# Linear attention into a two-of-four expert attention layer on one Trainium2 core: three batches in flight instead of two, with TensorE's instructions in program order

## The chip, the core and the metric

The kernel runs on one core of one Trainium2 chip. The metric is the device time of one execution in microseconds, less is better. The core has a matrix engine (TensorE: PE for matmuls and transposes, PEld for its weight loads), VectorE (DVE), ScalarE (ACT), GpSimd (POOL) and SyncE (SP), which here issues all the DMAs. [...] 

## The reference

Eight batches of 576 tokens. The first half is linear attention with 8 heads of 64, normalised per token and head; the second half is a mixture of four causal attention experts, of which each token uses the two with the largest logits.

```python
# q, k, v: (8, 8, 576, 64)
kv  = einsum('bhsd,bhse->bhde', k, v)
out = einsum('bhsd,bhde->bhse', q, kv)
x   = out / sqrt(mean(out*out, -1) + 1e-6) * g_norm      # -> (8, 576, 512)
logits = x @ w_gate                                      # 4 experts, the best 2 are kept
w = softmax over the two kept logits
for e in range(4):
    q, k, v = x @ wq[e], x @ wk[e], x @ wv[e]            # 512 -> 64
    a = causal_softmax(q @ k.T / 8)
    y += w[e] * (a @ v @ wo[e])                          # 0 where e was not kept
```

## The kernel before

The work goes batch by batch. The 576 tokens make five blocks, four of 128 and one of 64. Two Python generators emit a batch's instructions, and each `yield` is a place where the other generator may be advanced.

`stage1(b)` is the linear attention. `kv_pair` makes k^T v (`p_kv`, L179), `kv_copy` takes it from PSUM to SBUF (`kvx` on DVE, L187; `kv` on ACT, L188). `q_block` transposes q (`p_q`, L200, copied by DVE to `qT`, L205). The gate weights are folded into the same product (`p_kt`, `kvT`, `p_kg`). Then, block by block, `p_out` (L243) is q times kv; DVE copies it to `o_sb` (L250), ACT squares it (`sq`, L254), and DVE sums the squares per head (`ms`, L260). When all five blocks are done, DVE computes the reciprocal square root for all tokens at once, by a bit shift and four Newton steps of three small instructions each (L271 to L281). DVE forms the logits (`gl`, `lg`), and POOL multiplies the rows by the factor, one instruction per block (`x_tok`, L296). TensorE transposes each `x_tok` block (`p_x`, L307), and ACT copies it to `xT` (L312).

`stage2(b)` is the experts. It works out the gates on DVE (L322 to L341, with one ACT exponential), then `p_v` (L347, copied by DVE to `vext`), and for two pairs of experts the projections (`p_proj`, L365, cast by ACT to `qTp` and `kT`), the scores (`p_sc`, L393), their exponential on ACT (`PT`, L403), the causal mask on POOL (L408), the product with v (`p_O`, L445), the scaling by gate over row sum on DVE (`inv` and `osc`, L460 to L465), and the transposes of that (`p_OT`, L477, copied by ACT to `OT`). `final(b)` multiplies by wo (`p_y`, L501), ACT copies (`y`, L506) and SP stores (L507).

The matmul results share two sets of PSUM buffers: `big`, three of two banks (`p_out`, `p_proj`, `p_sc`, `p_O`), and `small`, two of one bank (`p_kv`, `p_q`, `p_kt`, `p_kg`, `p_x`, `p_v`, `p_OT`, `p_y`).

`weave` runs `stage2(b)` as the main stream and slips in `stage1(b + 1)` in proportion to costs that the generators yield. The part of `stage1` up to `p_out` is spread over 72% of `stage2`; the part from the normalisation on is held back to its last 8%. `final(b)` is emitted inside `stage2(b + 1)`. What the Python code emits is not yet the order of the engines: the framework's scheduler then orders each engine's instructions by readiness and priority. In the queues it makes, the normalisation of batch b + 1 and its `p_x` transposes stand between the last `p_O` of batch b and the first full `p_v` of batch b + 1.

The q, k and v tiles have two buffers; `load_qkv(b + 2)` is emitted at the start of round b. `kvx`, `lg8`, `ms` and `vext` also alternate between two copies; `o_sb` has one.

Of the kernel before, what the change touches and what calls it, by code (L numbers as in the profile page):

```python
# [10 lines left out]
FP32R = mybir.dt.float32r  # L11
BF16 = mybir.dt.bfloat16
# [6 lines left out]
def kernel(  # L19
# [13 lines left out]
    nc = tc.nc  # L33
    P = nc.NUM_PARTITIONS
    B, H, S, Dh = q.shape
    D = H * Dh
    E, _, Hd = moe_wq.shape
    assert (P, H, S, Dh, E, Hd) == (128, 8, 576, 64, 4, 64)
    NCH = D // P
# [25 lines left out]
    def small(shape, name, dtype=FP32):  # L65
        return ps1.tile(shape, dtype, tag="small", name=name)
# [121 lines left out]
            nc.scalar.copy(kv2[pp, :, hh * Dh : (hh + 1) * Dh], p_kv[pp, :, :])  # L188


    def stage1(b, res):
        qb, kb, vb = loads[b]
        qT = s1.tile([P, NCH, S], FP32, tag="qT", name="qT", bufs=1)
        kvb, kv2 = kvx[b % 2], kv2s[b % 2]
# [39 lines left out]
            q_block(i)  # L234
            yield 0.5

        xT = s1.tile([P, NCH, S], FP32R, tag="xT", name="xT")
        lg8, ms = lg8s[b % 2], mss[b % 2]

        for i, (t0, nt) in enumerate(blocks):  # L240
# [33 lines left out]
            out=y[:].bitcast(I32), in0=half[:], scalar1=-1.0, scalar2=float(0x5F3759DF),  # L274
            op0=AluOpType.mult, op1=AluOpType.add,
        )
        for it in range(4):
            u, w, y2 = tiny("u"), tiny("w"), tiny("y")
            nc.vector.scalar_tensor_tensor(out=u[:], in0=y[:], scalar=0.5, in1=y[:], op0=AluOpType.mult, op1=AluOpType.mult)
            nc.vector.tensor_tensor(out=w[:], in0=u[:], in1=m, op=AluOpType.mult)  # L280
            nc.vector.scalar_tensor_tensor(out=y2[:], in0=w[:], scalar=1.5, in1=y[:], op0=AluOpType.subtract, op1=AluOpType.mult)  # L281
            y = y2
        gl = blk.tile([P, NB * H, E], FP32, tag="gl", name="gl")
        nc.vector.tensor_tensor(
# [9 lines left out]
        for i, (t0, nt) in enumerate(blocks):  # L294
# [5 lines left out]
                op=AluOpType.mult,  # L300
            )
            xts.append(xt)
        yield 0.0
        for i, (t0, nt) in enumerate(blocks):
            p_x = small([P, NCH, P], "p_x")
            for c in range(NCH):
# [7 lines left out]
        res["xT"] = xT  # L314


    def stage2(b, res, prev_y):
        xT = res["xT"]
        lg8 = lg8s[b % 2]
        m8 = moe.tile([P, NB, 8], FP32, tag="m8", name="m8")  # L320
# [20 lines left out]
        nc.vector.tensor_tensor(out=gate[:], in0=gt[:], in1=rden[:].unsqueeze(2).to_broadcast([P, NB, E]), op=AluOpType.mult)  # L341

        vx = vexts[b % 2]
        for i, (t0, nt) in enumerate(blocks):
            p_v = small([P, E * Hd], "p_v")
            for c in range(NCH):
                nc.tensor.matmul(  # L347
                    p_v[:nt, :],
                    lhsT=xT[:, c, t0 : t0 + nt],
                    rhs=w_r["v"][:, c, :, :].rearrange("p e f -> p (e f)"),  # L350
                    start=(c == 0),
                    stop=(c == NCH - 1),
                )
            nc.vector.tensor_copy(  # L354
                out=vx[:nt, i, :, 0:Hd], in_=p_v[:nt].rearrange("p (e f) -> p e f", e=E)
            )
            yield 0.47

        def proj(pr):
            out_t = []  # L360
            for nm in ("q", "k"):
                p_p = big("p_proj")
                for c in range(NCH):
                    for s in range(2):
                        nc.tensor.matmul(  # L365
                            p_p[:, s, 0:HALF],
                            lhsT=w_r[nm][:, c, 2 * pr : 2 * pr + 2, :].rearrange("p e f -> p (e f)"),
                            rhs=xT[:, c, s * HALF : (s + 1) * HALF],
                            start=(c == 0),
                            stop=(c == NCH - 1),  # L370
                        )
                if nm == "q":
                    t = moe.tile([P, S], FP32R, tag="qTp", name="qTp", bufs=3)
                else:
                    t = kTs[(2 * b + pr) % 3]
                nc.scalar.copy(
                    t[:, 0:S].rearrange("p (s n) -> p s n", s=2), p_p[:, :, 0:HALF]
                )
                out_t.append(t)
                yield 1.0  # L380
            res["qk", pr] = out_t

        def scores(pr):
            qTp, kTp = res["qk", pr]
            PT = moe.tile([P, 2, strips], BF16, tag="PT", name="PT", bufs=3)

            def piece(parts):
                p_s = big("p_sc")
                o = 0
                for kb, lo, hi in parts:  # L390
                    for el in range(2):
                        pb = slice(el * Hd, (el + 1) * Hd)
                        nc.tensor.matmul(  # L393
                            p_s[:, el, o : o + hi - lo],
                            lhsT=kTp[pb, kb * P : (kb + 1) * P],
                            rhs=qTp[pb, lo:hi],
                            start=True,
                            stop=True,
                        )
                    o += hi - lo  # L400
                kb, lo, hi = parts[0]
                d0 = strip_off[kb] + lo - kb * P
                nc.scalar.activation(PT[:, :, d0 : d0 + o], p_s[:, :, 0:o], ACTF.Exp, scale=scale)  # L403

            def mask(kb):
                w = min(P, S - kb * P)
                d = PT[:w, :, strip_off[kb] : strip_off[kb] + w]
                nc.gpsimd.affine_select(  # L408
                    out=d, in_=d, compare_op=AluOpType.is_ge, fill=0.0, base=0,
                    pattern=[[0, 2], [1, w]], channel_multiplier=-1,  # L410
                )

            piece([(0, 0, HALF)])
            mask(0)
            yield 0.25
            piece([(0, HALF, S)])
            yield 0.25
            piece([(1, P, S)])
            mask(1)
            yield 0.35  # L420
            piece([(2, 2 * P, S)])
            mask(2)
            yield 0.25
            piece([(3, 3 * P, S), (4, 4 * P, S)])
            mask(3)
            mask(4)
            yield 0.2
            res["PT", pr] = PT

        OT = moe.tile([P, EP, S], BF16, tag="OT", name="OT")  # L430

        def pv(pr):
            PT = res["PT", pr]
            p_O = big("p_O")
            inv = moe.tile([P, NB, 2], FP32, tag="inv", name="inv")
            osc = moe.tile([P, NB, 2, Hd], BF16, tag="osc", name="osc")
            groups = ((0, (0, 1, 2)), (1, (3, 4)))
            for bank, qcs in groups:
                for n, qc in enumerate(qcs):
                    s0, nq = blocks[qc]  # L440
                    for el in range(2):
                        for kb in range(qc + 1):
                            nk = blocks[kb][1]
                            col = strip_off[kb] + s0 - kb * P
                            nc.tensor.matmul(  # L445
                                p_O[:nq, bank, (2 * n + el) * (Hd + 1) : (2 * n + el + 1) * (Hd + 1)],
                                lhsT=PT[:nk, el, col : col + nq],
                                rhs=vx[:nk, kb, 2 * pr + el, :],
                                start=(kb == 0),
                                stop=(kb == qc),  # L450
                            )
                    yield 0.11 * (qc + 1)
                for sub in ((qcs,) if bank == 0 else ((3,), (4,))):
                    nq = blocks[sub[0]][1]
                    n0, nn = sub[0] - qcs[0], len(sub)
# [12 lines left out]
                        in1=iv.rearrange("p n e -> p (n e)").unsqueeze(2).to_broadcast([nq, 2 * nn, Hd]),  # L468
                        op=AluOpType.mult,
                    )  # L470
            res["osc", pr] = osc

        def o_t(pr):
            osc = res["osc", pr]
            p_t = small([P, S], "p_OT", BF16)
            for qc, (s0, nq) in enumerate(blocks):
                nc.tensor.transpose(  # L477
                    p_t[:, s0 : s0 + nq],
                    osc[:nq, qc, :, :].rearrange("p e f -> p (e f)"),
                    ident_b[:nq, :nq],  # L480
                )
            nc.scalar.copy(OT[:, pr, :], p_t[:])  # L482
            yield 0.5

        yield from proj(0)
        yield from scores(0)
        yield from proj(1)
        yield from scores(1)
        if prev_y is not None:
            yield from prev_y  # L490
        yield from pv(0)
        yield from o_t(0)
        yield from pv(1)
        yield from o_t(1)
        res["OT"] = OT

    def final(b, OT):
        for qc, (s0, nq) in enumerate(blocks):
            p_y = small([P, D], "p_y")
# [8 lines left out]
            yield 0.45  # L508


    W1, W2 = 14.0, 14.3
    OUT_END = 11.6 / W1

    def target(a):
        if a < 0.92:
            return min(a / 0.72, 1.0) * OUT_END
        return 1.0

    def weave(main, side):
        a = s = 0.0  # L520
        live = side is not None
        for c in main:
            a += c / W2
            while live and s < target(a):
                try:
                    s += next(side) / W1
                except StopIteration:
                    live = False
        if live:
            for _ in side:  # L530
                pass

    res = {}
    for _ in stage1(0, res):
        pass
    y_gen = None
    for b in range(B):
        if b + 2 < B:
            loads[b + 2] = load_qkv(b + 2)
        nxt = {}  # L540
        weave(stage2(b, res, y_gen), stage1(b + 1, nxt) if b + 1 < B else None)
        y_gen = final(b, res["OT"])
        res = nxt
    for _ in y_gen:
        pass


# [28 lines left out]
```

## Time and profile before

| | |
|---|---|
| time, median of 3 runs | 362.43 us (361.71 to 363.38) |
| the profiled execution's own time | 362.53 us |
| its span, first to last instruction | 360.7 us |
| PE busy | 291.8 us (81%), 2616 instructions |
| PEld / DVE / ACT / POOL busy | 234.8 / 188.2 / 153.0 / 80.4 us |
| mean granted TensorE clock | 0.837 |
| moved by DMA | 40.30 MB, mean 112 GB/s |

The span is what the instructions take, the execution's own time is 1.8 us more. The profile gives for each group of instructions its busy time, and for idle time what ended it ("<-"). The granted clock is the share of TensorE's full speed that its throttle let through; a matmul's length is to be read together with it. Times inside the trace are counted from the start of the span.

### The profile page before, as it was taken

How to read it: one execution, taken by the hardware profiler on the slowest of the kernel's cores; microseconds unless marked ns; L12 is line 12 of the kernel's file. 1: busy time of each engine (PE TensorE's matmuls, PEld its weight loads, DVE VectorE, ACT ScalarE, POOL GpSimd, SP SyncE). 2: the span in 40 equal slices, each digit the busy share in tenths (PEclk: the TensorE clock that was granted, in tenths of full speed). 3: DMA queues.
4: the chain of work that ended last, by engine and by line, in shares of the span. 5: the costliest groups of instructions: out<-in, count | busy, mean ns of one | idle time of the engine just before them, and what ended most of it. 6: DMA issues, size and time to landing. Idle time of an engine off the chain costs nothing.

```text
span 360.7 us, 6721 instructions
## 1 busy us (share of the span) xinstructions
PE 291.8 (81%) x2616; PEld 234.8 (65%) x2624; DVE 188.2 (52%) x561; ACT 153.0 (42%) x273; POOL 80.4 (22%) x148
## 2 busy tenths in 40 slices
PE   2782898849994999949995899949996799949883
PEld 2581687638863788638964698638874598728551
DVE  0259654772458444781558444781458534783040
ACT  0202345432581336622572326722663326713833
POOL 8000602150220502150220502141210502132220
PEclk9997599977997599956998599966998589965966
DMA  7968999901737066600872056700002000300213
GB/s 218 214 167 222 241 266 263 207 16 45 220 89 176 2 207 135 185 0 13 250 177 87 2 159 164 195 11 2 2 37 93 2 2 0 133 1 2 88 45 132
DMA packets 75280, 40.30 MB, mean 112 GB/s; under 512 B 54000, under 2 KB 70384, under 8 KB 75248
## 3 DMA queue, kind: packets, MB, share of 16 engines
q1 hardware_dynamic: 75248, 39.86, 42.6%
q8 instruction: 21, 0.34, 0.4%
q14 instruction: 11, 0.09, 0.1%
HBM read 30.42 MB, written 9.44 MB: 110 GB/s over the span
## 4 chain that ended last, share of the span: by engine, by line
PE 56%; issue 22%; ACT 9%; POOL 5%; DVE 4%; DMA 1%; SPq 1%; DVEq 0%; ACTq 0%; POOLq 0%
PE p_proj L365 11%; PE p_x L307 10%; PE p_v L347 7%; PE p_kv L179 7%; PE p_q L200 5%; PE p_out L243 5%; ACT PT L403 4%; POOL x_tok L296 4%; PE p_sc L393 4%; PE p_kg L224 2%; PE p_y L501 2%; DVE o_sb L250 2%; DMA v_b<-in_v_dram 1%; POOL PT L408 1%; ACT y L506 1%
## 5 line engine op out<-in xcount | busy, mean ns | idle before, releaser
L307 PE MATMUL p_x<-ident_f,x_tok 128*128 128x128 f32 (+1 forms) x160 | 39.2, 411 | 39.2 <-POOL x_tok L296 38.1
L408 POOL TENSOR_SCALAR_AFFINE_SELECT PT<-PT 128x256 bf16<-128x256 bf16 (+1 forms) x80 | 29.9, 383 | 167.8 <-ACT PT L403 167.0
L296 POOL TENSOR_TENSOR x_tok<-o_sb,y 128x512 f32<-128x512 f32 (+1 forms) x40 | 42.1, 1083 | 96.7 <-DVE y L281 96.7
L403 ACT ACTIVATE PT<-p_sc 128x576 bf16<-128x576 f32 (+3 forms) x80 | 53.5, 712 | 17.7 <-PE p_sc L393 17.6
L307 PEld LDWEIGHTS p_x<-ident_f,x_tok 128*128 128x128 f32 (+1 forms) x160 | 26.9, 216 | 48.5 <-POOL x_tok L296 45.3
L243 PE MATMUL p_out<-kvx,qT 128*128 128x136 f32 (+1 forms) x320 | 45.8, 291 | 1.6 <-ACT PT L403 0.6
L243 PEld LDWEIGHTS p_out<-kvx,qT 128*128 128x128 f32 (+1 forms) x320 | 38.9, 182 | 6.3 <-ACT PT L403 3.3
L205 DVE COPY qT<-p_q 128x512 f32<-128x512 f32 (+1 forms) x40 | 24.8, 637 | 27.7 <-PE p_q L200 27.7
L354 DVE CAST vext<-p_v 128x256 bf16<-128x256 f32 (+1 forms) x40 | 17.0, 425 | 39.5 <-PE p_v L347 39.1
L254 ACT ACTIVATE sq<-p_out 128x512 f32<-128x512 f32 (+1 forms) x40 | 23.8, 595 | 27.8 <-DVE o_sb L250 19.2
L250 DVE COPY o_sb<-p_out 128x544 f32<-128x544 f32 (+1 forms) x40 | 28.8, 720 | 12.9 <-PE p_out L243 10.6
L260 DVE TENSOR_REDUCE ms<-sq 128x8 f32<-128x520 f32 (+1 forms) x40 | 27.3, 684 | 12.7 <-ACT sq L254 12.7
L445 PE MATMUL p_O<-vext,PT 128*128 128x65 bf16 (+2 forms) x480 | 29.1, 200 | 4.9 <-DVE osc L465 4.2
L179 PE MATMUL p_kv<-v_b,k_b 128*64 128x64 f32 x512 | 28.1, 275 | 6.0 <-DMA v_b<-in_v_dram 5.9
L445 PEld LDWEIGHTS <-PT 128*128 128x128 bf16 (+2 forms) x480 | 23.2, 103 | 13.8 <-issue 9.7
L179 PEld LDWEIGHTS p_kv<-v_b,k_b 128*64 128x64 f32 x512 | 25.2, 187 | 8.0 <-DMA k_b<-in_k_dram 4.5
L347 PE MATMUL p_v<-wv_r,xT 128*128 128x256 f32 (+1 forms) x160 | 30.4, 329 | 0.0
L312 ACT CAST xT<-p_x 128x512 fp32r<-128x512 f32 (+1 forms) x40 | 21.7, 543 | 18.0 <-PE p_x L307 17.9
L393 PE MATMUL p_sc<-qTp,kT 64*128 64x288 f32 (+2 forms) x192 | 25.0, 338 | 2.3 <-ACT PT L403 1.5
L347 PEld LDWEIGHTS p_v<-wv_r,xT 128*128 128x128 f32 (+1 forms) x160 | 25.0, 215 | 1.8
L365 PE MATMUL p_proj<-xT,wq_r 128*128 128x288 f32 x128 | 25.7, 321 | 0.3 <-ACT PT L403 0.3
L501 PE MATMUL p_y<-wo_b,OT 128*128 128x512 bf16 (+1 forms) x72 | 23.4, 409 | 1.8 <-ACT OT L482 1.4
(67 smaller groups left out, 370.5 us busy)
## 6 DMA issues: line engine op xcount, KB each, us to landing
q_b<-in_q_dram SPq DMA_DIRECT2D x32, 256.0 KB, 4.7
out_dram<-y SPq DMA_DIRECT2D x32, 256.0 KB, 2.0
k_b<-in_k_dram SPq DMA_DIRECT2D x7, 1024.0 KB, 5.8
v_b<-in_v_dram SPq DMA_DIRECT2D x7, 1024.0 KB, 8.6
k_b<-in_k_dram SPq DMA_DIRECT2D x4, 256.0 KB, 4.2
v_b<-in_v_dram SPq DMA_DIRECT2D x4, 256.0 KB, 4.5
k_rem<-in_k_dram SPq DMA_DIRECT2D x8, 128.0 KB, 8.5
v_rem<-in_v_dram SPq DMA_DIRECT2D x8, 128.0 KB, 7.5
```

The lines of the kernel that those rows point to most:

```text
L179: nc.tensor.matmul(p_kv[hh * Dh : (hh + 1) * Dh, c, :], lhsT=lk, rhs=rv, start=(j == 0), stop=(j == NF), skip_group_check=True,)
L243: nc.tensor.matmul(p_o[:nt, c // 2, (c % 2) * 2 * GW : (c % 2 + 1) * 2 * GW], lhsT=qT[:, c, t0 : t0 + nt], rhs=kvb[:, c, :, :].rearrange(" ...
L250: nc.vector.tensor_copy(out=ob[:nt, i].rearrange("p (k h) g -> p k (h g)", k=2), in_=p_o[:nt, :, 0 : 4 * GW])
L296: nc.gpsimd.tensor_tensor(out=xt[:nt], in0=ob[:nt, i, :, 0:Dh], in1=y[:nt, i * H : (i + 1) * H].unsqueeze(2).to_broadcast([nt, H, Dh]), op ...
L307: nc.tensor.transpose(p_x[:, c, :nt], xts[i][:nt, 2 * c : 2 * c + 2, :].rearrange("p h d -> p (h d)"), ident_f[:nt, :nt],)
L347: nc.tensor.matmul(p_v[:nt, :], lhsT=xT[:, c, t0 : t0 + nt], rhs=w_r["v"][:, c, :, :].rearrange("p e f -> p (e f)"), start=(c == 0), stop= ...
L365: nc.tensor.matmul(p_p[:, s, 0:HALF], lhsT=w_r[nm][:, c, 2 * pr : 2 * pr + 2, :].rearrange("p e f -> p (e f)"), rhs=xT[:, c, s * HALF : (s ...
L393: nc.tensor.matmul(p_s[:, el, o : o + hi - lo], lhsT=kTp[pb, kb * P : (kb + 1) * P], rhs=qTp[pb, lo:hi], start=True, stop=True,)
L403: nc.scalar.activation(PT[:, :, d0 : d0 + o], p_s[:, :, 0:o], ACTF.Exp, scale=scale)
L408: nc.gpsimd.affine_select(out=d, in_=d, compare_op=AluOpType.is_ge, fill=0.0, base=0, pattern=[[0, 2], [1, w]], channel_multiplier=-1,)
L445: nc.tensor.matmul(p_O[:nq, bank, (2 * n + el) * (Hd + 1) : (2 * n + el + 1) * (Hd + 1)], lhsT=PT[:nk, el, col : col + nq], rhs=vx[:nk, kb ...
L501: nc.tensor.matmul(p_y[:nq, :], lhsT=OT[:, pr, s0 : s0 + nq], rhs=wo_b[:, pr, :], start=(pr == 0), stop=(pr == EP - 1),)
```

## The change

`stage1` is cut in two. `stage_a` goes from `p_kv` to `x_tok`; `stage_x` holds only the `p_x` transposes and their copies to `xT`. `stage2` becomes `stage_s`. Round b now merges three streams: `stage_s(b)`, `stage_x(b + 1)` and `stage_a(b + 2)`. Inside `stage_s` the pieces are put in a written order. All of it stands in a block that keeps TensorE's instructions in the order in which they are emitted; the other engines are still ordered by the scheduler. The Newton steps go from four to three, with the sign handled by `reverse0`. Loads are emitted three batches ahead.

```diff
-    def stage1(b, res):
+    def stage_a(b, res):
...
-        for it in range(4):
+        for it in range(3):
...
-            nc.vector.scalar_tensor_tensor(out=y2[:], in0=w[:], scalar=1.5, in1=y[:], op0=AluOpType.subtract, op1=AluOpType.mult)
+            nc.vector.scalar_tensor_tensor(
+                out=y2[:], in0=w[:], scalar=1.5, in1=y[:], op0=AluOpType.subtract, op1=AluOpType.mult, reverse0=True
+            )
...
-        yield 0.0
+        res["x_tok"] = xts
+
+
+    def stage_x(res):
+        xts = res["x_tok"]
+        xT = s1.tile([P, NCH, S], FP32R, tag="xT", name="xT")
...
-    def stage2(b, res, prev_y):
+    def stage_s(b, res, prev_y):
...
-        yield from proj(0)
-        yield from scores(0)
-        yield from proj(1)
-        yield from scores(1)
-        if prev_y is not None:
-            yield from prev_y
-        yield from pv(0)
-        yield from o_t(0)
-        yield from pv(1)
-        yield from o_t(1)
...
+        st = {"V": v_proj(), "Q0": proj(0), "Q1": proj(1), "S0": scores(0), "S1": scores(1)}
+        st.update({"P0": pv(0), "P1": pv(1), "T0": o_t(0), "T1": o_t(1), "Y": prev_y})
+        order = (
+            "Q0 Q0 V V S0 V S0 V S0 V S0 Q1 S0 Q1 S1 Y S1 Y S1 P0 P0 P0 S1 P0 P0 S1 Y T0 Y Y P1 P1 P1 P1 P1 T1"
+        )
...
-    W1, W2 = 14.0, 14.3
...
+    def merge(*streams):
+        live = [[t0, t0, (t1 - t0) / cost, gen] for gen, cost, t0, t1 in streams if gen is not None]
+        while live:
+            x = min(live, key=lambda x: x[0])
+            try:
+                x[0] += next(x[3]) * x[2]
+            except StopIteration:
+                live.remove(x)
+
+    CA, CX, CS = 11.8, 2.25, 14.5
+    with tc.manual_schedule(engines={mybir.EngineType.PE}):
+        res = [dict() for _ in range(B)]
+        merge((stage_a(0, res[0]), CA, 0.0, 1.0))
+        loads[2] = load_qkv(2)
+        merge((stage_x(res[0]), CX, 0.3, 0.6), (stage_a(1, res[1]), CA, 0.0, 1.0))
+        y_gen = None
+        for b in range(B):
+            if b + 3 < B:
+                loads[b + 3] = load_qkv(b + 3)
+            merge(
+                (stage_s(b, res[b], y_gen), CS, 0.0, 1.0),
+                (stage_x(res[b + 1]) if b + 1 < B else None, CX, 0.05, 0.4),
+                (stage_a(b + 2, res[b + 2]) if b + 2 < B else None, CA, 0.1, 1.0),
+            )
+            y_gen = final(b, res[b]["OT"])
+        for _ in y_gen:
+            pass
```

More of the change, by code (lines that the diff above doesn't have):

```diff
@@ L235, in stage1 @@
             yield 0.5
-        xT = s1.tile([P, NCH, S], FP32R, tag="xT", name="xT")
         lg8, ms = lg8s[b % 2], mss[b % 2]
@@ L343, in stage2, with v_proj @@
         vx = vexts[b % 2]
[L344 to L352, printed above, removed]
-                )
[L354 to L357, printed above, removed]
+        def v_proj():
+            for i, (t0, nt) in enumerate(blocks):
+                p_v = small([P, E * Hd], "p_v")
+                for c in range(NCH):
+                    nc.tensor.matmul(
+                        p_v[:nt, :],
+                        lhsT=xT[:, c, t0 : t0 + nt],
+                        rhs=w_r["v"][:, c, :, :].rearrange("p e f -> p (e f)"),
+                        start=(c == 0),
+                        stop=(c == NCH - 1),
+                    )
+                nc.vector.tensor_copy(
+                    out=vx[:nt, i, :, 0:Hd], in_=p_v[:nt].rearrange("p (e f) -> p e f", e=E)
+                )
+                yield 0.47
         def proj(pr):
-            out_t = []
+            out_t = res["qk", pr] = []
             for nm in ("q", "k"):
@@ L380, in proj @@
                 yield 1.0
-            res["qk", pr] = out_t
         def scores(pr):
             qTp, kTp = res["qk", pr]
-            PT = moe.tile([P, 2, strips], BF16, tag="PT", name="PT", bufs=3)
+            PT = res["PT", pr] = moe.tile([P, 2, strips], BF16, tag="PT", name="PT", bufs=3)
             def piece(parts):
@@ L427, in scores @@
             yield 0.2
-            res["PT", pr] = PT
-        OT = moe.tile([P, EP, S], BF16, tag="OT", name="OT")
+        OT = res["OT"] = moe.tile([P, EP, S], BF16, tag="OT", name="OT")
         def pv(pr):
@@ L435, in pv @@
             inv = moe.tile([P, NB, 2], FP32, tag="inv", name="inv")
-            osc = moe.tile([P, NB, 2, Hd], BF16, tag="osc", name="osc")
+            osc = res["osc", pr] = moe.tile([P, NB, 2, Hd], BF16, tag="osc", name="osc")
             groups = ((0, (0, 1, 2)), (1, (3, 4)))
@@ L451, in pv @@
                             )
-                    yield 0.11 * (qc + 1)
+                    if qc != qcs[-1]:
+                        yield 0.11 * (qc + 1)
                 for sub in ((qcs,) if bank == 0 else ((3,), (4,))):
@@ L470, in pv @@
                     )
-            res["osc", pr] = osc
+                yield 0.11 * (qcs[-1] + 1)
         def o_t(pr):
@@ L483, in o_t @@
             yield 0.5
-        yield from proj(0)
-        yield from scores(0)
-        yield from proj(1)
-        yield from scores(1)
-        if prev_y is not None:
-            yield from prev_y
-        yield from pv(0)
-        yield from o_t(0)
-        yield from pv(1)
-        yield from o_t(1)
-        res["OT"] = OT
+        st = {"V": v_proj(), "Q0": proj(0), "Q1": proj(1), "S0": scores(0), "S1": scores(1)}
[3 more added lines that the diff above has]
+        )
+        for key in order.split():
+            if st[key] is not None:
+                yield next(st[key])
+        for g in st.values():
+            assert g is None or next(g, None) is None
     def final(b, OT):
@@ L508, in final @@
             yield 0.45
-    W1, W2 = 14.0, 14.3
[L512 to L545, printed above, removed]
+    def merge(*streams):
[20 more added lines that the diff above has]
+                (stage_a(b + 2, res[b + 2]) if b + 2 < B else None, CA, 0.1, 1.0),
+            )
+            y_gen = final(b, res[b]["OT"])
+        for _ in y_gen:
+            pass
 _INS = ['q', 'k', 'v', 'g_norm', 'moe_w_gate', 'moe_wq', 'moe_wk', 'moe_wv', 'moe_wo']
```

## The prediction

> **What bounds it now.** I read the page first, then the waits, then the timeline of one batch, then its stretches with the granted clock. TensorE is the busiest engine, and twice per ten slices or so its busy digit and its clock sag together:
>
> ```profile
> PE 291.8 (81%) x2616; PEld 234.8 (65%) x2624; DVE 188.2 (52%) x561; ACT 153.0 (42%) x273; POOL 80.4 (22%) x148
> PE   2782898849994999949995899949996799949883
> PEclk9997599977997599956998599966998589965966
> ```
>
> The waits (engine, line, awaited: total us, times, longest) name the sag. The transposes of x wait for POOL once per batch:
>
> ```profile
> PE p_x L307 <- POOL x_tok L296: 38.1, 9, 8.0
> PE p_O L445 <- DVE osc L465: 4.2, 7, 0.7
> PE p_OT L477 <- DVE osc L465: 4.1, 9, 0.8
> ```
>
> The timeline of one seam (start, length, engine, line) shows the chain behind it:
>
> ```profile
> 230.98 1.14 PE L243 MATMUL p_out<-kvx,qT 128*64 128x136 f32 x8
> 232.46 0.71 DVE L250 COPY o_sb<-p_out 64x544 f32<-64x544 f32 x1
> 233.26 0.59 ACT L254 ACTIVATE sq<-p_out 64x512 f32<-64x512 f32 x1 [1.65 <-DVE inv L460]
> 234.83 0.67 DVE L260 TENSOR_REDUCE ms<-sq 64x8 f32<-64x520 f32 x1
> 236.24 0.17 DVE L271 TENSOR_SCALAR half<-ms 128x40 int32<-128x40 int32 x1
> ...
> 239.65 3.21 POOL L296 TENSOR_TENSOR x_tok<-o_sb,y 128x512 f32<-128x512 f32 x3 [9.93 <-DVE y L281]
> 240.88 1.48 PE L307 MATMUL p_x<-ident_f,x_tok 128*128 128x128 f32 x5 [4.30 <-POOL x_tok L296]
> ```
>
> From the end of the last p_out (232.05) to the first p_x (240.88) are 8.8 us. PE covers part of that with p_O and p_OT, and idles 0.65 + 0.45 + 4.30 = 5.4 us. Then the clock. Stretches of 3.41 us laid on the clock's own steps (length, busy PE, PEld, DVE, ACT, POOL, granted clock, DMA) and one whole period:
>
> ```profile
> 229.65:233.06 3.41, 3.41 (x48) 2.31 (x46) 3.27 (x7) 1.96 (x4) 0.06 (x1) 1.00 0.59 217
> 233.06:236.47 3.41, 2.32 (x33) 1.71 (x31) 2.47 (x15) 0.59 (x1) 0.00 (x0) 1.00 0.28 66
> 236.47:239.88 3.41, 0.10 (x1) 0.00 (x0) 3.10 (x19) 0.64 (x1) 0.23 (x1) 0.50 0.00 0
> 239.88:243.29 3.41, 2.41 (x10) 1.81 (x11) 3.04 (x12) 0.98 (x3) 3.41 (x4) 0.50 0.00 0
> 243.29:246.70 3.41, 3.23 (x19) 2.50 (x17) 0.57 (x2) 2.13 (x4) 1.57 (x2) 0.50 0.01 2
> 246.70:250.11 3.41, 3.41 (x44) 3.19 (x45) 0.43 (x1) 0.37 (x1) 0.00 (x0) 0.50 0.02 5
> 250.11:253.52 3.41, 3.41 (x63) 3.24 (x59) 1.28 (x4) 0.72 (x2) 0.00 (x0) 0.99 0.00 0
> ...
> 198.65:239.65 41.00, 35.18 (x327) 28.53 (x328) 22.87 (x70) 18.90 (x34) 8.94 (x16) 0.83 0.43 117
> ```
>
> The clock falls at 236.47, after a stretch with PE busy 2.32 of 3.41, and returns at 250.11, only after a stretch that is full of real matmuls. PE works 9.0 us at half clock and so loses 4.5. A batch of 41.0 us is therefore 41.0 - 5.4 - 4.5 = 31.1 us of PE at full clock. DVE (22.9), ACT (18.9), POOL (8.9) and the DMA (share 0.43) are well below that: a pipeline without the seam would be worth ten us a batch.
>
> **Does the change remove the seam?** I compared the instruction queues of the two programs. In the new one the queue of PE at each seam reads p_out of the last block, five p_OT, one p_proj (8 matmuls), then p_x. Stage_a(b + 2) ends with its round and stage_x(b + 2) starts at 0.05 of the next. So behind the last p_out PE has only p_OT (0.45 us) and one p_proj (218.47 to 219.64, 1.2 us) before it stands at p_x; since the order is fixed, p_proj of k, 40 p_kv and all p_v are queued behind that wait though their inputs are ready. DVE's queue at that place holds p_O's scaling before the last o_sb. The new chain, from the end of the last p_out:
> - DVE's queue from the o_sb of block 3 on: o_sb 0.64, ms 0.60, inv 0.15, ms 0.65, inv 0.13, osc 0.50, steps of two more osc 0.71, together 3.4. It starts as p_out of block 3 ends; PE takes 24 p_O (0.055 each) and p_out (1.1), 2.4, to the end of the last p_out. DVE is late by 1.0
> - o_sb 0.65, then sq 0.1 + 0.6, then ms 0.70: 2.05
> - half, y and nine Newton steps at the 0.232 spacing seen at 238 to 239: 2.55. One step of three (0.70) is gone; that is the gain of the shorter iteration, and `reverse0` adds none, the instruction being the same (200 ns)
> - x_tok 1.15 and the hop 0.1: 1.25
>
> Sum 6.9 us, 1.9 less than before. PE covers 1.65, so it idles 5.3 us against 5.4. The seam has moved inside the round; it has not gone.
>
> **The other terms of a period.**
> - Small PSUM waits. Behind p_x come p_kv and then two p_v on two `small` buffers. p_kv's buffer is free only after DVE, ACT, DVE, ACT (0.43, 0.37, 0.43, 0.37), with ACT doing an xT of 0.58 first; the two p_v wait 0.75 and 0.6. Later p_kg waits for kvT, a p_out for its buffer, p_OT for osc: some 0.85 together. The old queue had 0.3 of this. Bounds 1.0 and 3.5; I take 2.2, the sum of those hops.
> - Clock. The idle time puts one step of 3.41 us far below 2.32 us busy, so the clock falls. After p_x come p_proj and p_kv, 3.5 us of real matmuls, 7 at half clock, in place of five p_x. So the full stretch ends between 1.1 + 3.4 and 1.1 + 6.8 us after the restart, on average at 6.2: 3.1 lost, between 2.25 and 4.0, less 0.4 that falls in the p_v waits.
> - The gates (gl to gate, 4.0 us on DVE) now stand ahead of kvx. They end 2.8 us after the restart, p_kv 4.0: free, with 1.2 of cover; without it every us is a us of p_v.
> - SP: the loads, a batch earlier, pass the output stores. A gain is excluded, since no PE wait of a steady period names a DMA; a load behind one store costs at most that store's issue, 0.4. I take 0: the share is 0.43 and k_b is needed a round later.
>
> Period 31.1 + 5.3 + 2.2 + 3.1 - 0.4 = **41.3**, between 39 and 44, against 41.0.
>
> [...] Here the clock fell with gaps of 0.65 and 0.45 in the stretch before, so I go by the row. [...]
>
> **Ends of the program.** Before: the first p_x at 37.1, seven periods (40.4 to 41.0), then 37.9 to the end. After, two batches are prepared first. p_out of batch 0 ends at 29.1. The next in PE's queue is p_kv of batch 1, ahead of p_x: it waits for the remainders of k and v, issued at 33.41 and 34.08 and 3.8 to 3.9 us on their way, until 38; at half clock 4.1 us of it are left, so 42.1. Then twelve users of the two `small` buffers (p_x, p_q, p_kt, p_kg), each 0.5 to 1.0 on PE and 0.8 in copy and hop, by twos: 11.5, so 53.7. Five p_out take 5.3 at full clock and 10.5 at half; I take 6.5, as real matmuls soon bring the clock back. Then the chain without osc, 2.05 + 2.55 + 1.25 = 5.9: first p_x of batch 1 near **66**, bounds 63 and 68. Round 0 has no p_y (10 matmuls of 0.29): 38.4. Then five periods. The last two rounds have no stage_a. From p_x of batch 7: x 2.3, round 6 16.0, round 7 17.2 and the last p_y, with half clock (4), two waits for osc a round (5 in all) and ACT's exponentials (2): 46.5; then the final block, which took 8.2 from the last OT: **55**, bounds 51 and 59.
>
> Sum 66 + 38.4 + 5 x 41.3 + 55 = 365.9 us of span. The profiled execution took 362.53, 1.8 more than its span, and stands 0.1 above the median: **368 us**. Before was 362.4. Half a per cent, 1.8 us, is about what a measurement of this kernel can tell from no change.
>
> **Rivals.**
> 1. *The waits behind p_x are absorbed and the clock returns early.* The copies run beside transposes at half clock and half the small waits vanish (1.2), and the restart falls well on the clock's steps (2.0 lost). Then 31.1 + 5.3 + 1.0 + 2.0 - 0.1 = 39.3 a period, and with the lower ends 63 + 36.4 + 196.5 + 51 + 1.8 = 349 us: faster. For it: the old PE has no wait between 209 and 230. Against: there the scheduler had filled them. It decides from a period under 40.5. Chance 0.27.
> 2. *The clock stays low one step longer.* The stretch from 243.29, busy 3.23 with transposes in it, did not raise it; p_x and the p_v waits now stand among the matmuls. Each period then loses 1.7 more, seven times: 380 us. Chance 0.14.
> 3. *The change does what it says.* If x_tok came in time, no idle, clock full: 31.1 + 2.2 a period, 63 + 30.4 + 166.5 + 50 + 1.8 = 312 us. The queue order speaks against it; only a chain under 2 us would do, and Newton alone is 2.55. Chance 0.05.
>
> **The numbers.** My own case has 0.54 and a range of 358 to 378; of it 0.39 is slower by over half a per cent, 0.09 within, 0.06 faster. With the rivals: faster 0.27 + 0.05 + 0.06 = 0.38, same 0.09, slower 0.39 + 0.14 = 0.53. The range of 8 in 10 reaches into both neighbours: 348 to 384; outside are rival 3 and the tails of 1 and 2.
>
> **What would show it.** Right: p_x still waits for POOL 3 us or so a batch and p_OT for DVE 2 us; the distance from one first x_tok to the next stays 40 to 43; mean clock 0.80 to 0.87; new PE waits at p_v, together 1 us or more a batch; first p_x of batch 1 near 66. [...]

## The result, and the profile after

The changed kernel takes 385.86 us (median, 385.26 to 388.64) against 362.07 us before: a ratio of 1.068, 95% interval 1.061 to 1.075. It is slower, as forecast, but by 6.8% (6.6% by the medians) where 1.6% was expected, and outside the range of 348 to 384 us. Times here are medians of all runs, ratios compare means and leave out a run that is over 1.5% above the fastest of its kernel. The profiled execution took 385.58 us with a span of 383.5.

The page says that it is not a matter of more work: the span grew by 22.8 us, PE's busy time by 5.7 (291.8 to 297.5), and the mean clock is higher than before (0.869 against 0.837).

```profile
span 383.5 us, 6710 instructions
PE 297.5 (78%) x2624; PEld 236.9 (62%) x2624; DVE 188.8 (49%) x537; ACT 155.5 (41%) x273; POOL 80.5 (21%) x148
PEclk9997796999889975999569995899759995798997
```

The waits of TensorE (awaited: total us, times, longest) show one that was small before: p_O for osc, 4.2 us in 7 times, 0.7 at most. It is now nearly as long as the wait at p_x, which has fallen from 38.1 to 23.6:

```profile
PE p_x L313 <- POOL x_tok L297: 23.6, 7, 5.7
PE p_O L451 <- DVE osc L472: 22.7, 15, 2.8
PE p_OT L484 <- DVE osc L472: 5.8, 12, 1.0
PE p_v L355 <- ACT xT L318: 4.0, 6, 0.7
```

The timeline of one period shows where it stands, first at the first expert pair, then at the seam (PE and DVE rows; in brackets the idle time ahead and what ended it):

```profile
261.20 0.40 PE L451 MATMUL p_O<-vext,PT 128*128 128x65 bf16 x8 [0.98 <-DVE osc L472]
...
267.68 0.36 PE L451 MATMUL p_O<-vext,PT 128*128 128x65 bf16 x6
267.88 1.17 PE L242 MATMUL p_out<-kvx,qT 128*128 128x136 f32 x8
268.89 0.35 PE L451 MATMUL p_O<-vext,PT 128*128 128x65 bf16 x6
...
269.15 0.72 DVE L249 COPY o_sb<-p_out 128x544 f32<-128x544 f32 x1 [0.88 <-PE p_out L242]
269.80 0.69 DVE L259 TENSOR_REDUCE ms<-sq 128x8 f32<-128x520 f32 x1
270.40 0.19 DVE L467 RECIPROCAL inv<-p_O 128x6 f32<-128x6 f32 x1
270.60 0.69 DVE L259 TENSOR_REDUCE ms<-sq 128x8 f32<-128x520 f32 x1
...
271.40 0.56 DVE L472 TENSOR_TENSOR osc<-p_O,inv 128x384 bf16<-128x384 f32 x1
272.02 1.34 PE L451 MATMUL p_O<-vext,PT 128*128 128x65 bf16 x18 [2.78 <-DVE osc L472]
273.29 2.07 PE L242 MATMUL p_out<-kvx,qT 128*64 128x136 f32 x8
276.44 0.23 PE L484 MATMUL p_OT<-ident_b,osc 64*128 64x64 bf16 x1 [0.54 <-DVE osc L472]
276.60 2.29 PE L373 MATMUL p_proj<-xT,wq_r 128*128 128x288 f32 x8
281.44 0.90 PE L313 MATMUL p_x<-ident_f,x_tok 128*128 128x128 f32 x3 [2.56 <-POOL x_tok L297]
```

The first 12 p_O of the second expert pair are done at 269.2. The other 18 wait until DVE has scaled those 12 (osc), and DVE has an o_sb and two ms to do first. The last p_out, which starts the chain to x_tok, is queued behind these 18. It also runs at half clock (0.50 in the stretches below), 2.07 us in place of 1.14. What stands behind the wait at p_x waits with it, too: the p_proj of k, which reads the same xT as the p_proj at 276.60, starts only after p_x, at 282.21. In the kernel before, the last p_out (from 230.98 us) stood ahead of the p_O that waited, and at the seam the short wait held up only p_O and p_OT:

```profile
232.05 1.72 PE L445 MATMUL p_O<-vext,PT 128*128 128x65 bf16 x30
234.69 0.37 PE L445 MATMUL p_O<-vext,PT 128*128 128x65 bf16 x7 [0.65 <-DVE osc L465]
```

The stretches laid on the clock's steps (length, busy PE, PEld, DVE, ACT, POOL, clock, DMA) and one period, from the first x_tok of a batch to the first of the next:

```profile
265.90:269.31 3.41, 3.33 (x32) 2.65 (x31) 1.79 (x4) 2.56 (x5) 0.00 (x0) 1.00 0.40 154
269.31:272.73 3.42, 0.71 (x13) 0.58 (x12) 2.60 (x6) 0.60 (x1) 0.00 (x0) 0.99 0.17 38
272.73:276.14 3.41, 3.17 (x18) 2.40 (x17) 1.52 (x7) 0.00 (x0) 0.00 (x0) 0.50 0.00 0
276.14:279.55 3.41, 2.45 (x9) 2.04 (x9) 2.58 (x12) 1.74 (x3) 0.00 (x0) 0.50 0.01 2
279.55:282.96 3.41, 1.52 (x7) 1.52 (x8) 2.76 (x12) 0.38 (x2) 2.75 (x3) 0.50 0.02 5
282.96:286.37 3.41, 3.41 (x43) 3.13 (x43) 1.02 (x4) 0.98 (x3) 2.46 (x3) 0.50 0.00 0
235.75:280.21 44.46, 36.53 (x328) 29.40 (x328) 22.86 (x67) 19.13 (x34) 8.95 (x15) 0.85 0.08 27
```

The p_O wait leaves PE 0.71 us busy in the step from 269.31; the clock falls at its end, ahead of the seam, and stays at half for four steps, as many as before. PE is busy 10.55 us of these and loses 5.3. The period is 44.5 us.

### The profile page after: what moved, and what is told of

Read it like the earlier page. It is cut to its first block, busy times and chain, and to the rows that moved or that the text cites. A ratio compares the mean times of both kernels' runs of the same rounds, so it can differ in the third digit from the quotient of the medians.

```text
span 383.5 us, 6710 instructions
## 1 busy us (share of the span) xinstructions
PE 297.5 (78%) x2624; PEld 236.9 (62%) x2624; DVE 188.8 (49%) x537; ACT 155.5 (41%) x273; POOL 80.5 (21%) x148
## 4 chain that ended last, share of the span: by engine, by line
PE 49%; issue 27%; DVE 11%; ACT 5%; POOL 4%; DMA 1%; SPq 1%; DVEq 0%; ACTq 0%; POOLq 0%
PE p_proj L373 9%; PE p_sc L400 6%; PE p_x L313 6%; PE p_kv L179 6%; PE p_v L355 6%; PE p_q L200 4%; POOL x_tok L297 4%; PE p_y L506 4%; PE p_O L451 3%; PE p_out L242 3%; DVE osc L472 2%; PE p_kg L224 2%; DVE o_sb L249 2%; DVE qT L205 1%; DMA v_b<-in_v_dram 1%
## 5 line engine op out<-in xcount | busy, mean ns | idle before, releaser
L410 ACT ACTIVATE PT<-p_sc 128x576 bf16<-128x576 f32 (+3 forms) x80 | 56.2, 708 | 19.4 <-PE p_sc L400 17.9
L242 PE MATMUL p_out<-kvx,qT 128*128 128x136 f32 (+1 forms) x320 | 51.1, 313 | 0.0
L451 PE MATMUL p_O<-vext,PT 128*128 128x65 bf16 (+2 forms) x480 | 30.1, 198 | 22.8 <-DVE osc L472 22.7
L313 PE MATMUL p_x<-ident_f,x_tok 128*128 128x128 f32 (+1 forms) x160 | 28.3, 306 | 25.1 <-POOL x_tok L297 23.6
L242 PEld LDWEIGHTS p_out<-kvx,qT 128*128 128x128 f32 (+1 forms) x320 | 44.4, 197 | 3.9 <-ACT sq L253 2.1
L313 PEld LDWEIGHTS p_x<-ident_f,x_tok 128*128 128x128 f32 (+1 forms) x160 | 19.0, 157 | 31.1 <-POOL x_tok L297 25.8
L205 DVE COPY qT<-p_q 128x512 f32<-128x512 f32 (+1 forms) x40 | 25.1, 634 | 25.4 <-PE p_q L200 25.4
L179 PE MATMUL p_kv<-v_b,k_b 128*64 128x64 f32 x512 | 28.5, 277 | 10.3 <-DMA v_b<-in_v_dram 10.3
L400 PE MATMUL p_sc<-qTp,kT 64*128 64x288 f32 (+2 forms) x192 | 35.1, 372 | 1.5 <-ACT kT L384 1.5
L355 PE MATMUL p_v<-wv_r,xT 128*128 128x256 f32 (+1 forms) x160 | 29.0, 306 | 6.3 <-ACT xT L318 4.0
L355 PEld LDWEIGHTS p_v<-wv_r,xT 128*128 128x128 f32 (+1 forms) x160 | 21.0, 182 | 12.1 <-ACT xT L318 7.0
L373 PE MATMUL p_proj<-xT,wk_r 128*128 128x288 f32 x128 | 27.7, 374 | 0.0
L187 DVE COPY kvx<-p_kv 64x256 f32<-64x256 f32 x16 | 6.8, 422 | 42.2 <-PE p_kv L179 34.2
```

The costliest lines, as they stand in the source:

```text
L179: nc.tensor.matmul(p_kv[hh * Dh : (hh + 1) * Dh, c, :], lhsT=lk, rhs=rv, start=(j == 0), stop=(j == NF), skip_group_check=True,)
L205: nc.vector.tensor_copy(out=qT[:, :, t0 : t0 + nt], in_=p_q[:, :, :nt])
L242: nc.tensor.matmul(p_o[:nt, c // 2, (c % 2) * 2 * GW : (c % 2 + 1) * 2 * GW], lhsT=qT[:, c, t0 : t0 + nt], rhs=kvb[:, c, :, :].rearrange(" ...
L313: nc.tensor.transpose(p_x[:, c, :nt], xts[i][:nt, 2 * c : 2 * c + 2, :].rearrange("p h d -> p (h d)"), ident_f[:nt, :nt],)
L355: nc.tensor.matmul(p_v[:nt, :], lhsT=xT[:, c, t0 : t0 + nt], rhs=w_r["v"][:, c, :, :].rearrange("p e f -> p (e f)"), start=(c == 0), stop= ...
L373: nc.tensor.matmul(p_p[:, s, 0:HALF], lhsT=w_r[nm][:, c, 2 * pr : 2 * pr + 2, :].rearrange("p e f -> p (e f)"), rhs=xT[:, c, s * HALF : (s ...
```

## The experiments

My theory after the result was that one term was left out of the sum: the wait of the second p_O group for osc, 2.78 + 0.98 = 3.76 us a period, together with the earlier fall of the clock that it causes. The rivals were that DVE's queue is late whatever PE does, and that TensorE in a fixed order finds a new wait for each one taken away. Ratios are to the kernel before, run beside each. The two single edits, the filling and the free order have two runs each, the other three four.

**Scaling after both groups.** DVE's reads of the first group are emitted ahead of the matmuls of the second, and both groups write one PSUM tile. I took this to be why the framework makes the second group wait; the edit moves the reads behind both groups:

```diff
                     if qc != qcs[-1]:
                         yield 0.11 * (qc + 1)
+                if bank == 0:
+                    yield 0.11 * (qcs[-1] + 1)
+            for bank, qcs in groups:
                 for sub in ((qcs,) if bank == 0 else ((3,), (4,))):
...
-                yield 0.11 * (qcs[-1] + 1)
+            yield 0.11 * 5
```

> The changed kernel with one edit: the scaling of p_O on VectorE (inv, osc) is emitted after all five blocks of p_O and not after the first three, so that the matmuls of the second group are no longer behind osc of the first. Theory A (the term that I left out is this wait: p_O waited 22.7 us for osc, 2.78 and 0.98 us a round, held the last p_out behind it, and let the clock fall early): the p_O wait is gone, a period falls from 44.5 us to 40.5 to 42, the time from 386 to 364 to 374. Theory B (VectorE's queue is what is late, the wait only shows it): the wait turns up again at p_OT or p_x, a period stays above 43, the time above 378.

368.77 us, ratio 1.019 (1.013 to 1.026). Its waits:

```profile
PE p_OT L487 <- DVE osc L475: 25.4, 36, 1.4
PE p_x L313 <- POOL x_tok L297: 21.1, 7, 5.7
```

A period of it, from x_tok to x_tok:

```profile
226.58:267.45 40.87, 34.26 (x328) 27.19 (x328) 22.58 (x67) 19.34 (x34) 8.96 (x16) 0.92 0.09 30
```

The p_O wait is gone from the list, and 17 us with it; period and time are theory A's. But most of the wait returns at p_OT (5.8 to 25.4), as theory B had it: all that TensorE waits for osc fell only from 28.5 to 25.4 us. Of the 3.6 us by which the period is shorter, idle time makes 1.3 (7.9 to 6.6) and PE's busy time 2.3 (36.5 to 34.3), because the clock is low for two steps a period (184.35 to 191.18) and not four. By these figures the edit took away more half clock than waiting. That time and period come near the 368 and 41.3 of the prediction is not a match of its terms: of the 3.3 us a period that p_OT waits here its sum had less than 0.85.

**The transposes of x later.**

```diff
-                (stage_x(res[b + 1]) if b + 1 < B else None, CX, 0.05, 0.4),
+                (stage_x(res[b + 1]) if b + 1 < B else None, CX, 0.35, 0.7),
```

> The changed kernel with one edit: the transposes of x stand at 0.35 to 0.7 of a round and not at 0.05 to 0.4. Theory A (p_x stands too early, its wait is worth its idle time of about 3 us a round plus part of the half clock after it; the p_O wait stays): the p_x wait is gone, p_O still waits for osc about 3.7 us a round, a period is 37.5 to 40.5, the time 340 to 358. Theory B (the wait is only moved, since ScalarE and the PSUM buffers in the middle of the round are as late): a period above 42.5, the time above 372.

356.60 us, ratio 0.985 (0.979 to 0.992). The time is theory A's, at its upper end; the period, 41.05 us, is above A's 40.5 and below B's 42.5. p_x no longer waits for POOL; the p_O wait is as it was:

```profile
PE p_O L451 <- DVE osc L472: 22.4, 14, 2.8
```

A period:

```profile
216.83:257.88 41.05, 35.80 (x330) 28.82 (x330) 23.20 (x67) 19.26 (x34) 8.94 (x16) 0.87 0.09 30
```

The clock still falls at p_O. It stays at half for three steps a period (248.63 to 258.88) in place of four. Of the 29 us against the changed kernel 7 are won in round 0 alone (38.7 to 31.5).

**Both.**

> Both edits together. Theory A (two waits and the clock that they let fall are all that separates a period from 31.1 us of matrix work plus 1 to 2.5 us of small waits): no clock fall at the seam, granted clock above 0.95 from 70 us on, a period of 32.5 to 35, the time 305 to 326. Theory B (in-order TensorE loses the time to other waits as soon as these are gone): period above 37, time above 335.

344.51 us, ratio 0.951 (0.946 to 0.956): my range (305 to 326) failed, theory B was right. The period is 38.1 us, and the wait at the head of TensorE's list is the one that the first edit had left at p_OT:

```profile
PE p_OT L487 <- DVE osc L475: 25.4, 36, 1.4
```

Its two rows at a seam, and two steps of the clock there:

```profile
242.97 0.23 PE L487 MATMUL p_OT<-ident_b,osc 128*128 128x128 bf16 x1 [1.34 <-DVE osc L475]
244.18 0.20 PE L487 MATMUL p_OT<-ident_b,osc 64*128 64x64 bf16 x1 [0.98 <-DVE osc L475]
...
241.16:244.57 3.41, 1.08 (x9) 0.62 (x8) 3.21 (x13) 0.74 (x2) 0.00 (x0) 1.00 0.01 2
244.57:247.98 3.41, 3.41 (x16) 3.40 (x15) 3.00 (x17) 1.13 (x2) 1.35 (x2) 0.50 0.02 5
```

The p_OT of a pair wait for the scaling of that pair, 1.34 and 0.98 us at the seam. That leaves PE 1.08 of 3.41 busy, and the clock falls for a step or two though no single gap is longer than 1.34.

**One Newton step less in the old kernel.** The kernel before with `range(3)` and `reverse0`, nothing else.

> The kernel before with one edit: three Newton steps in place of four. The chain from ms to x_tok ends at the seam with TensorE idle, so one step is worth its three instructions, 0.70 us a batch: theory A 362 - 8 x 0.70 = 356.5 us, period 41.0 to 40.3. Theory B (the clock moves in steps of 3.41 us, so that the return of the full clock does not come earlier when the work does): half of it or nothing, 359 to 362.

348.77 us, ratio 0.964 (0.960 to 0.969): 13 us, more than double the 5.6 of theory A; B had half of that or nothing. Two periods of it:

```profile
151.99:190.04 38.05, 32.81 (x328) 26.43 (x328) 21.64 (x67) 18.72 (x34) 8.94 (x15) 0.90 0.47 125
190.04:230.39 40.35, 35.27 (x328) 28.58 (x328) 21.65 (x67) 18.89 (x34) 8.94 (x16) 0.84 0.44 118
```

Most seams now have two low steps (74.39 to 81.22) and not four, and are followed by a period of 37.5 to 38.4; two still have four, and 40.2 to 40.4 follow. With four low steps the period is 0.7 us below the 41.0 of before, the DVE time alone; the rest is the clock's steps. In the old kernel this part of the change is a gain by itself; in the new one it was not tried alone.

**Filling the waits.** 24 matmuls that nobody reads ahead of each first p_x, 16 ahead of the second p_O group of the second pair:

```diff
+    def fill(n):
+        p_f = small([P, E * Hd], "p_fill")
+        for j in range(n):
+            nc.tensor.matmul(p_f[:], lhsT=..., rhs=..., start=True, stop=True)
...
             if i == 0:
+                fill(24)
...
+                if pr == 1 and bank == 1:
+                    fill(16)
```

> The changed kernel with work added that nobody reads: 24 matmuls of two weight tiles (256 columns) ahead of each batch's first p_x, 16 ahead of the second group of p_O of the second pair, the two places where TensorE waits longest. Nothing else changes, the two waits stay. Theory A (beside its two waits a period loses about 5 us because the clock falls in them and stays at half for four steps of 3.41 us): the clock stays at full for most of the period, the stretch after the restart costs 2.5 us less and the last p_out 1 us less, period 44.5 to 40.5 to 41.5, the time 357 to 368, though 280 to 320 matmuls were added. Theory B (only the waits cost, the clock is a sign of them): no gain, 384 to 396.

369.39 us, ratio 1.024 (1.016 to 1.032). In the slices from 73 to 330 us (9.17 us each) the clock is at 0.9 or more; the page's row:

```profile
PEclk9976799899999999999999999999999999998998
```

A period:

```profile
184.59:225.75 41.16, 36.87 (x370) 30.32 (x369) 23.48 (x67) 19.11 (x34) 8.94 (x15) 1.00 0.44 116
```

The period, 41.2 us, is in theory A's range; the time is 1.4 above it, and round 0, which had little to win, got 1.6 longer. What waits for what is untouched, the added matmuls only take up part of the waiting (p_O 22.7 to 10.6, p_x 23.6 to 8.6), and with 320 more matmuls the kernel is 16 us faster. So the clock is a cost in itself, 3.3 us a period, and not only a sign of the waits.

**TensorE ordered by the scheduler.**

```diff
-    with tc.manual_schedule(engines={mybir.EngineType.PE}):
+    if True:
```

> The changed kernel without the fixed order of TensorE: the scheduler orders it again; emission, the three batches and three Newton steps stay. Theory A (the fixed order puts p_x and the second group of p_O ahead of work that is ready, and that is what costs): the scheduler moves ready work ahead, the p_O wait falls to 1 us a round or less, the time is 335 to 365. Theory B (three batches in flight in themselves cost, by PSUM and VectorE queues): 375 or more.

326.21 us, ratio 0.904 (0.895 to 0.913), below even theory A's range. The same emission, the same three batches. Its waits at the places in question:

```profile
PE p_x L313 <- POOL x_tok L297: 3.9, 3, 2.7
PE p_O L451 <- DVE osc L472: 0.2, 1, 0.2
```

A period:

```profile
205.26:241.90 36.64, 34.01 (x328) 27.64 (x328) 23.16 (x67) 18.77 (x35) 8.80 (x15) 0.95 0.10 33
```

Against the changed kernel, holding TensorE to the written order costs 60 us. Against the kernel before the gain is 35 us; 13 of these the three Newton steps gave there alone, so some 22, if the two add up, are an estimate of what three batches and the new emission bring. The waits that I walked into by the written order are those that the scheduler goes round.

**A better written order.** Both edits, and p_OT behind other work (`T0` after two blocks of `P1`, the second pair's, `T`, in the next round). Of the diff the order alone:

```diff
-            "Q0 Q0 V V S0 V S0 V S0 V S0 Q1 S0 Q1 S1 Y S1 Y S1 P0 P0 P0 S1 P0 P0 S1 Y T0 Y Y P1 P1 P1 P1 P1 T1"
+            "Q0 Q0 V T V S0 V S0 V S0 V S0 Q1 S0 Q1 S1 Y S1 Y S1 P0 P0 P0 S1 P0 P0 S1 Y Y Y P1 P1 T0 P1 P1 P1"
```

> Both edits of before (scaling last, x at 0.35 to 0.7) and p_OT moved behind other work: the first pair's after two blocks of the second p_O, the second pair's into the next round behind p_v. In the run with both edits TensorE still waited 25.4 us for osc at p_OT, 3.35 us a round, and the clock fell there for one or two steps. Theory A (that wait and its clock are what is left): no wait over 0.6 us in a period, the clock stays up, period 38.1 to 32.5 to 34.5, the time 303 to 322. Theory B (another wait takes its place, PSUM or the chain to x_tok): period above 36, time above 330.

318.09 us, ratio 0.880 (0.873 to 0.887), the fastest here, ahead of both kernels. PE and its clock from the page:

```profile
PE 273.9 (87%) x2624; PEld 216.9 (69%) x2624; DVE 181.6 (57%) x537; ACT 157.2 (50%) x273; POOL 80.4 (25%) x148
PEclk9999579999996699999999999999999999999985
```

A period:

```profile
166.39:200.18 33.79, 32.14 (x335) 25.74 (x332) 21.78 (x67) 19.45 (x34) 8.92 (x16) 1.00 0.52 141
```

Time and period, 33.8, are in theory A's range, with the clock at full and PE idle for 1.65 us of that period; one seam (the fall at 97.5 us) still went low for three steps, and the end of the program is low again. So a fixed order need not be a loss: it costs what stands in it too early. Whether the scheduler would do better still with this emission was not tried.

## Why the prediction was right and wrong

The direction was right, but mostly for another reason. Of the 5.2 us of span that were forecast, 3.7 came from the ends of the program and 1.5 from five periods; of the 22.8 measured, with the old period of 41.0 as the measure, the ends make 5.3 and the five periods 17.5. The ends were right: first p_x of batch 1 at 64.73 (forecast 66), round 0 38.7 us (38.4), from the first p_x of batch 7 at 325.88 to the end 57.6 us (55). Right was also that the new p_x stands behind one p_proj and waits for POOL; moving it away is worth 29 us. Rivals 1 and 3 did not come about. Rival 2 came near in time (380) by a mechanism that was not there: the clock is low for four steps, but it does return within 4.9 us of the restart at 281.44, inside the 4.5 to 7.9 that was given; the other steps lie ahead of the restart.

What failed is the period, 44.5 us against 41.3 (bounds 39 and 44); the five full ones alone make 16 of the 17.6 us by which the sum of the span was short. The step that failed is the first one below, a wait that the sum put at nothing. Its terms:

- *The step "PE takes 24 p_O (0.055 each) and p_out (1.1), 2.4"* had no wait in it. Measured, from the end of p_out 3 to the end of the last p_out: 6.3 us, with 2.78 of wait and p_out at half clock. With 0.98 in the first pair, this wait is 3.76 us. It was in front of me: the row "p_O <- DVE osc: 4.2, 7, 0.7" stands among the waits that the prediction shows. Before, its price at the seam was 0.65; in the new DVE queue an o_sb and two ms come first, and the prediction adds up that queue (3.4 us) beside PE's 2.4 as if the two ran side by side, without asking who waits for a piece in its middle.
- *The clock*, 3.1 less 0.4, was 5.3 us. After the restart it cost 2.5, close to the estimate. The other 2.8 lie ahead of it, since the p_O wait lets the clock fall before the last p_out; I had counted only what comes after p_x.
- *The seam* was put at 5.3 us of idle time and is 0.54 + 2.56. DVE is not late at the last o_sb, because PE is later still; the chain from the last p_out to p_x is 6.1 us, not 6.9, and PE covers more of it at half clock.
- *The small waits* were put at 2.2 us. Other than p_O and the seam, p_v alone is left: 0.67 + 0.38, against 0.75 + 0.6.

Sum of the measured terms: 31.1 + 3.1 + 3.8 + 1.0 + 5.3 = 44.3, for 44.5. It was luck that the period was not missed by more: 6.4 us too little for the p_O wait and the clock stood against 3.4 too much for the seam and the small waits. Two readings were also slightly off: PE's time in the four half-clock rows is 9.15 us and not 9.0, and the seven periods before run from 40.3 to 41.1.

The period was also missed by about one step of the clock. Where the clock falls once in a period, its falls lie whole steps of 3.41 us apart in the traces: 12 steps (40.96 us) before from 113.62 on, 13 (44.37) in the changed kernel from 139.57 on, 12 again in both single edits, and 11 or 12 in the old kernel with three Newton steps. That each single edit gives a period of 41, though they take away different waits, is thus no measure of either wait.

The length of a gap does not decide alone whether the clock falls. It fell after a gap of 2.78, in the run with both edits after gaps of 1.34 and 0.98, and before after 0.65 and 0.45 (the fall at 236.47); PE was busy for 0.71, 1.08 and 2.32 us of these steps. How long PE is busy in a step does not decide alone either. The step before with 2.32 us, most of it p_O and p_OT, ended in a fall; in the run with the scaling after both groups a step with 1.79 us (from 99.02 us), idle from 100.8 on, did not, and in the better written order the clock stayed at half after a step with PE busy throughout (3.41 us, from 97.50). What decides it is not shown by these runs.

## What to carry to other kernels

Before an engine's order is fixed by hand, go through its queue and ask for every instruction that waits how long its awaited engine's own queue is at that moment. A wait that a reordering scheduler goes round becomes, in a fixed order, the wait of all that stands behind it: at p_O and p_x 22.7 and 23.6 us here, against 0.2 and 3.9 with the scheduler. Emit the reads of a result tile after the last writes to it where the framework would otherwise put the later writes behind the reads; here that was worth 17 us. Where the granted clock moves in steps, as it did here by 3.41 us, the price of a wait is its length plus the steps it lets fall (5.3 of the 44.5 us of a period here were lost at half clock), and a small gain on the chain at a seam can be worth double, as the Newton step was in the old kernel (13 us for 5.6).

## What was not expected of the hardware

- In the traces of both kernels the granted clock changed only on a grid of 3.41 us, between 1.00 and 0.50: in the changed kernel the stretches at one clock last from 3.41 us (one step, from 344.37) to 34.13 (ten, 67.89 to 102.02). In the other runs, looked at in windows of 0.25 us, the falls and returns seen are whole steps apart too. In the old kernel shortening a chain by 0.70 us took 13 us off eight batches, because in most seams two low steps fell away.
- Matmuls whose result is never read, put into waits, made the changed kernel 4% faster (385.86 to 369.39 us).
- Not a matter of the chip, and open: that the second p_O group waits because both groups share one PSUM tile was not tried by giving them two. Shown is only that the wait goes when the reads are emitted later.
